# First-batch x by gathers of 128 rows, table zero fill on Scalar, and the second batch's first folds inside the first chunk

## The chip, the cores and the metric

The kernel runs on one core of one Trainium2 chip. The metric is the device time of one execution in microseconds (us), taken as the median over runs of the same program. Engines are named as in the profile: PE (TensorE, PEld its weight loads), DVE (VectorE), ACT (ScalarE), POOL (GpSimd) and SP (SyncE), which here only issues transfers. Transfers issued by SP and ACT go through hardware queues, those of POOL through a software queue.

## The reference

A Fourier mixing of x (8 batches, 3008 positions, 256 channels; the real part of a two-dimensional FFT over positions and channels), then a two-layer perceptron with a hard-swish in between.

```
X = np.fft.fft(x, axis=1)
X = np.fft.fft(X, axis=2)
x2 = X.real.reshape(B * S, D)
h = x2 @ w_in                       # 256 -> 2048
g = h * np.clip(h + 3.0, 0.0, 6.0) / 6.0
out = g @ w_out                     # 2048 -> 256
```

x is float32; both weights arrive as float64.

## The kernel before

**Tiling.** The FFT over 3008 = 47 x 64 positions is done in two stages of matmuls. Stage 1 transforms over the 47 rows. Because the transform of a real signal has symmetric and antisymmetric parts, x is first *folded*: a forward tile and a tile of mirrored partner rows are added (`fold_half`, `fold`), part 0 over the positions and part 1 over the channels. Stage 1's results z go to DRAM (`zd`, and a column `zq`) and come back in another layout as g; stage 2 multiplies g with a table T and gives q, which feeds the perceptron. One row of q is broadcast over the partitions through DRAM (`spread_half`, tile qn).

Batches go in pairs. The first pair is cut into two `Half` objects, `halves[0]` and `halves[1]`, one per batch, so that the first batch can start early. A half has four tiles m, taken in `ORDER` = 3, 0, 1, 2. Each has a forward tile `hb.x[m]` and a partner tile `hb.xr[m]`; the upper and lower 64 partitions hold two groups of columns, 47 rows each. The partner rows come by an indirect transfer, `gather`, whose row numbers lie in the integer tile IX (cast from the float tile FI). Forward rows come by two plain transfers of 64 or 48 rows each. Tile 3 is special: it has the last column group, and one more plain transfer wraps to column 0.

**Start.** Before the main loop the program clears buffers, loads the tables F, C, T and the first pieces of weights, makes float32 of the float64 weights, and does stage 1 of the first batch. Weights come in 16 pieces of 512 KB (`load_w`). `exponent_a` (ACT), `exponent_b` (a PE matmul) and `exponent_c` (ACT) make a piece's exponents, `mantissa` (DVE, two operations) its mantissa, and `join` (DVE) multiplies them. `fold_w_in` multiplies a w_in piece with the channel transform C on PE, ACT copies the result to W1, and SP copies one row of it to WN. `keep_awake` issues matmuls without use on PE. After the first two pieces come the four tiles of the first batch: `fold_half` on DVE, `stage1_early` on PE, copies of z by ACT. The half-empty diagonal blocks of T are zeroed by two memsets on POOL, and in tiles 0, 1, 2 a strip of partitions 32 to 63 is cleared by ACT before the load fills 47 rows of it, so that the rows that no transfer fills hold numbers.

Each engine executes its instructions in the order in which the program issues them; nothing reorders them. POOL's transfers use eight completion semaphores in turn, so each waits for the transfer eight before it; the hardware queues have a rotation of their own.

**Main loop.** The loop runs over `steps`: pair, chunk `ck` (12 per pair), and `fc` from 0 to 7. In each step PE does the first layer for a later step (`mlp1`, L520), DVE and ACT the activation (L529 to L569), POOL the sums `c` for the second layer (`combine`, three operations at L583 by a helper), and PE the second layer (`mlp2`, L613, three products with `a` and four with `c`), in a scheme with seven products of G blocks in place of eight. In the first chunk (`s` < 8) the weights are not ready, so `first_steps` and `second_steps` mix the weight work with the steps, and the second layer runs with eight products (`mlp2_first`, L593) that need no POOL. `mix_w_out(i)` on POOL makes the mixed G blocks for the second chunk on; it overwrites a block that `mlp2_first` reads.

**Background work.** `beside(p)` lists by hand what else is done at which step: `ahead` items are issued at the start of a step, `behind` items after `mlp1`. For pair 0 these are table loads, g loads, `stage2_half`, `spread_half`, the mixes, and all of the second batch: `take_half` and `load_half` (plain transfers on SP, gather on POOL), `fold_half` on POOL, and `stage1_quarters` on PE.

Pools are rings of buffers: `xpool` (4 buffers, also used by some weight pieces), `ypool` (2), `zpool` (2), `cpool` (3), `qpool` and `apool`.

Of the kernel before, what the change touches and what calls it, by code (L numbers as in the profile page):

```python
# [7 lines left out]
F32 = mybir.dt.float32  # L8
# [50 lines left out]
def kernel(  # L59
# [29 lines left out]
    NH = N2 // 2 + 1  # L89
    NG = NCK // 2  # L90
    NSG = 4
    DH = 32
    assert S == N1 * N2 and D == 2 * P and B % 2 == 0 and TB == 256 and NK1 % (2 * KK) == 0

# [19 lines left out]
    ctx.enter_context(tc.manual_schedule())  # L114

    F = consts.tile([P, 7 * PB], F32, name="F")
    FI = consts.tile([P, NP * NXC + 1], F32, name="FI")
    IX = consts.tile([P, NP * NXC], I32, name="IX")
    T = consts.tile([P, 2, NG, 2, 2 * KK, N2], F32, name="T")
    C = consts.tile([P, 2, D], F32, name="C")  # L120
    W1 = consts.tile([P, 2, FF], F32, name="W1")
# [15 lines left out]
    ORDER = [NM - 1] + list(range(NM - 1))  # L137

    def x_tile(pool=xpool, tag="x"):
        return pool.tile([PX, XC, D], F32, tag=tag, name="xt")  # L140

# [23 lines left out]
        pr.xr[c] = xr  # L167
        gather(xr, pr.p * NXC + c)

    def gather(xr, i):  # L170
        nc.gpsimd.indirect_dma_start(
            out=xr[0:PX].rearrange("p n d -> p (n d)"), out_offset=None, in_=x_r,
            in_offset=bass.IndirectOffsetOnAxis(ap=IX[0:PX, i:i + 1], axis=0),
        )

    class Half:
# [6 lines left out]
    def take_half(hb, m, pool=xpool, tag="x"):  # L183
        hb.x[m], hb.xr[m] = x_tile(pool, tag), x_tile(pool, tag)

    def load_half(hb, m, queue, gap=False):
        for h in range(2):
            c = m + h * NM
            nr = N1 + 1 if h or gap else PB
            n = XC if c < NXC - 1 else XC - 1  # L190
            rows, o = x_pn[hb.b * N1:hb.b * N1 + nr], hb.x[m][h * PB:h * PB + nr]
            queue.dma_start(out=o[:, 0:n, :], in_=rows[:, c * XC + 1:c * XC + 1 + n, :])
            if n < XC:
                queue.dma_start(out=o[:, n:XC, :], in_=rows[:, 0:1, :])
        gather(hb.xr[m], hb.b * NM + m)

    def fold_half(hb, m, part, eng):
        xt, xr = hb.x[m][0:PX - 1], hb.xr[m][0:PX - 1]
# [101 lines left out]
    def stage1_early(hb, m):  # L300
# [26 lines left out]
                    nc.tensor.matmul(ps[h][i * PB:(i + 1) * PB, :, to], table(t, h), y[rows(h), 2 * i:2 * i + 2, fr],  # L327
                                     start=(k == 0), stop=(k > 1), skip_group_check=True)
        k = ORDER.index(m)
        pool, tag = (zpool, "z") if k < 2 else (cpool, "c")  # L330
        z = pool.tile([PX, 2, 2, D + 1], F32, tag=tag, name="z")
        for h in range(2):
            nc.scalar.copy(z[:, h, :, D:], pt[h][0:PX])
# [13 lines left out]
    def stage1_quarters(hb, m):  # L347
        y = hb.y.pop(m)
        cosine, sine = slice(0, P + 1), slice(P + 1, D)
        ps = [bank([P, 2, D], "ps1"), ps_h.tile([P, 2, D], F32, tag="uv", name="ps1")]  # L350
        for i in range(2):
            for h in range(2):
                o = ps[h][i * PB:(i + 1) * PB]
                end = m == NM - 1 and h and i
                n = 1 if end else 2
                nc.tensor.matmul(o[:, 0:n], table(0, h), y[rows(h), 2 * i:2 * i + n], start=True, stop=not end,
                                 skip_group_check=True)
                for k, (j, cs) in enumerate([(XC - 1, cosine), (XC, cosine), (XC - 1, sine), (XC, sine)] if end else ()):
                    nc.tensor.matmul(o[:, 1, cs], table(k + 1, h), y[rows(h), j, cs], start=False, stop=(k % 2 == 1),
                                     skip_group_check=True)  # L360
        z = zpool.tile([PX, 2, 2, D], F32, tag="z", name="z")
        for h in range(2):
            nc.scalar.copy(z[:, h], ps[h][0:PX])
        zc = zpool.tile([PX, 2, 2], F32, tag="zc", bufs=4, name="zc")
        nc.scalar.activation(zc[:], z[:, :, :, P], AF.Identity, scale=FI[0:PX, NP * NXC:])
        if hb.b not in first.zd:
            first.zd[hb.b] = dpool.tile([NG, 2 * KK, 2, NS, D], F32, tag="zd1", name="zd")
            first.zq = dpool.tile([NG, 2 * KK, 2, NS], F32, tag="zq0", name="zq")
        zd, zq = first.zd[hb.b], first.zq
        for i in range(2):  # L370
            r = slice(i * PB, i * PB + PZ)
            for h in range(2):
                n0 = (m + h * NM) * XC + 2 * i
                end = m == NM - 1 and h and i
                n = 1 if end else 2
                nc.sync.dma_start(out=zd[:].rearrange("g k c n d -> (g k c) n d")[:, n0:n0 + 2, 0:D], in_=z[r, h])
                nc.sync.dma_start(out=zq[:, :, ::-1, n0:n0 + n].rearrange("g k c n -> (g k) c n"), in_=zc[r, h, 0:n])
                if end:
                    nc.sync.dma_start(out=zq[:, :, :, n0 + 1].rearrange("g k c -> (g k c)"), in_=z[r, h, 1, P])

    def turn_column(pr, c, z):
        zc = zpool.tile([PB + PZ, 2, 2], F32, tag="zc", bufs=4, name="zc")
        nc.scalar.activation(zc[:].rearrange("p n b -> p b n"), z[:, :, :, P], AF.Identity,
                             scale=FI[0:PB + PZ, NP * NXC:])
        for h in range(2):
            n = 1 if (c, h) == (NXC - 1, 1) else 2
            cs = slice(c * XC + 2 * h, c * XC + 2 * h + n)
# [441 lines left out]

    clear_bytes(0)  # L830
    nc.vector.memset(half[:], 0.5)
    nc.vector.tensor_copy(IX[:], FI[:, 0:NP * NXC])
    clear_bytes(1)
    clear_bytes(2)
    for k, m in enumerate(ORDER):
        take_half(hb, m, *((xpool, "x"), (xpool, "x"), (qpool, "q"), (apool, "a"))[k])
        if k:
            gap = hb.x[m][PB // 2:PB].rearrange("p n d -> p (n d)")
            nc.scalar.copy(gap.rearrange("p (i n) -> p i n", i=2), Z[PB // 2:PB].unsqueeze(1).to_broadcast([PB // 2, 2, 2 * TB]))

    def head(j):
        exponent_a(j)
# [20 lines left out]
                            channel_multiplier=1)  # L863
    nc.scalar.mul(E[:, 1], E[:, 0], -1.0)
    for k, m in enumerate(ORDER):
        load_half(hb, m, nc.gpsimd, gap=k > 0)
    for j in range(2, 4):
        load_w(j)
    for b in range(2):
        nc.gpsimd.memset(T[(1 - b) * N2:(2 - b) * N2, b].rearrange("p g a k n -> p (g a k n)"), 0.0)  # L870
    load_t(0)
    for j in range(2):
        exponent_a(j)
        mantissa(j)
        exponent_b(j)
        keep_awake(1)
    for j in range(2):
        tail(j)
        fold_w_in(j)
    keep_awake(1)  # L880
    for k, m in enumerate(ORDER):
        for part in range(2):
# [29 lines left out]
    def beside(p):  # L912
# [7 lines left out]
        if p == 0:  # L920
# [3 lines left out]
            put(4, stage2_half, halves[0], 1)  # L924
            put(5, spread_half, halves[0], 1)
            put(NF - 1, close_w)
            for i, t in enumerate((4, 6, 8, 9)):
                put(t, mix_w_out, i)
            for gr in range(2, NSG):
                put(8 * gr - 10, load_g_half, halves[0], gr)  # L930
# [2 lines left out]

            hb = halves[1]
            for k, m in enumerate(ORDER):
                t = 9 + 3 * k
                put(t - 3, take_half, hb, m)
                put(t - 3, load_half, hb, m, nc.sync)
                for part in range(2):
                    put(t + part, fold_half, hb, m, part, nc.gpsimd)  # L940
                put(t + 3, stage1_quarters, hb, m, at=behind)
            for gr in range(NSG):
                put(8 * gr + 23, load_g_half, hb, gr)
                put(8 * gr + 27 - (gr == 0), stage2_half, hb, gr)
# [132 lines left out]
def _tables(B, S, D):  # L1077
# [21 lines left out]

    npc = N2 // 8  # L1100
    row = np.zeros((128, B // 2, npc))
    for i in range(B):
        r = ((i * N1 + np.arange(N1)[::-1, None]) * 2 + 2) * npc - 1
        for h in range(2):
            if i > 1:
                row[i % 2 * 64:i % 2 * 64 + N1, i // 2] = r - np.arange(npc)
            else:
                row[h * 64:h * 64 + N1, 0, i * npc // 2:(i + 1) * npc // 2] = r - np.arange(npc // 2) - h * npc // 2
    sign = 1.0 - 2.0 * (np.arange(128)[:, None] % 2)
    f = np.concatenate([f1.reshape(128, -1), row.reshape(128, -1), sign], axis=1)  # L1110

    k = k1[:, None] + N1 * np.arange(N2)
    n2 = np.arange(N2 // 2) + 1
# [42 lines left out]
```

## Time and profile before

| | |
|---|---|
| median of 3 runs | 1953.43 us (1951.49 to 1958.76) |
| profiled execution | 1953.19 us, of it span 1951.5 us |
| granted PE clock over the span | 0.998 |
| PE busy | 1928.2 us (99%) |
| DVE busy | 1424.0 us (73%) |
| ACT busy | 678.2 us (35%) |
| POOL busy | 1440.9 us (74%) |
| read from and written to DRAM | 58.27 and 37.32 MB |
| PE waiting for POOL's `c` (L583), whole span | 2.6 us in 2 waits |
| POOL waiting for the first g (`see`) | 16.4 us in 1 wait |

The span is one execution taken by the profiler; the run's time lies 1.7 us above it. Busy time is an average over stages with different limits, so what a change in one stage is worth is read from that stage's own rows. Times within the span are counted from its start. A matmul in float32 is recorded as two instructions, so the counts of PE rows are twice those of the code.

### The profile page before, as it was taken

How to read it: one execution, taken by the hardware profiler on the slowest of the kernel's cores; microseconds unless marked ns; L12 is line 12 of the kernel's file. 1: busy time of each engine (PE TensorE's matmuls, PEld its weight loads, DVE VectorE, ACT ScalarE, POOL GpSimd, SP SyncE). 2: the span in 40 equal slices, each digit the busy share in tenths (PEclk: the TensorE clock that was granted, in tenths of full speed). 3: DMA queues.
4: the chain of work that ended last, by engine and by line, in shares of the span. 5: the costliest groups of instructions: out<-in, count | busy, mean ns of one | idle time of the engine just before them, and what ended most of it. 6: DMA issues, size and time to landing. Idle time of an engine off the chain costs nothing.

```text
span 1951.5 us, 28212 instructions
## 1 busy us (share of the span) xinstructions
PE 1928.2 (99%) x9354; PEld 1655.9 (85%) x9354; DVE 1424.0 (73%) x2754; ACT 678.2 (35%) x1166; POOL 1440.9 (74%) x1649
## 2 busy tenths in 40 slices
PE   8999999999999999999999999999999999999997
PEld 4678888888998888888898888888899888888887
DVE  4876776767777777777787777777778777777777
ACT  4633333333333333333333333333333333333322
POOL 4278888886677887787678887878667667666765
PEclk9999999999999999999999999999999999999999
DMA  6432223311112122121111221112110101101000
GB/s 179 153 86 65 67 52 91 77 47 35 34 33 55 44 68 73 40 55 27 41 32 46 57 57 42 51 50 54 35 28 20 28 17 26 30 17 28 19 19 20
DMA packets 154408, 97.43 MB, mean 50 GB/s; under 512 B 122035, under 2 KB 136174, under 8 KB 154262
## 3 DMA queue, kind: packets, MB, share of 16 engines
q1 hardware_dynamic: 143106, 59.71, 12.7%
q0 software_dynamic: 10448, 35.69, 6.6%
q8 instruction: 73, 1.20, 0.3%
q14 instruction: 73, 0.60, 0.1%
q10 hardware_dynamic: 708, 0.23, 0.1%
HBM read 58.27 MB, written 37.32 MB: 49 GB/s over the span
## 4 chain that ended last, share of the span: by engine, by line
PE 94%; DVE 2%; ACT 1%; POOL 1%; DMA 1%; issue 1%; DVEq 0%; ACTq 0%; POOLq 0%
PE acc L613 56%; PE v L520 16%; PE u L520 16%; PE ps L469 2%; PE ps L270 1%; PE acc L593 1%; DVE a L569 1%; PE awake L811 1%; ACT t L566 0%; DMA st<-in_moe_w_in_dram 0%; DVE s L529 0%; PE spare L794 0%; PE ps L327 0%; DVE o L674 0%; DVE u L550 0%
## 5 line engine op out<-in xcount | busy, mean ns | idle before, releaser
L583 POOL TENSOR_TENSOR c<-a 128x512 f32<-128x512 f32 (+1 forms) x375 | 468.3, 1249 | 370.4 <-PE acc L613 309.5
L613 PE MATMUL acc<-c,G 128*128 128x256 f32 (+1 forms) x3008 | 697.9, 375 | 2.7 <-POOL c L583 2.6
L566 ACT ACTIVATE t<-u,half 128x512 f32<-128x512 f32 (+1 forms) x384 | 260.8, 679 | 1144.5 <-DVE u L539 1065.3
L613 PEld LDWEIGHTS acc<-c,G 128*128 128x128 f32 x3008 | 564.9, 190 | 75.6 <-POOL c L583 4.7
L529 DVE SCALAR_TENSOR_TENSOR s<-qn,WN,u 128x256 f32<-128x256 f32 (+1 forms) x768 | 330.6, 472 | 346.5 <-PE u L520 342.0
L613 PE MATMUL acc<-a,G 128*128 128x256 f32 (+1 forms) x2256 | 541.8, 376 | 0.0
L613 PEld LDWEIGHTS acc<-a,G 128*128 128x128 f32 x2256 | 421.8, 190 | 72.9 <-issue 20.2
L520 PE MATMUL v<-q,W 127*128 127x256 f32 (+1 forms) x1536 | 389.4, 375 | 2.0 <-DVE a L569 2.0
L520 PE MATMUL u<-q,W 128*128 128x256 f32 (+1 forms) x1536 | 388.0, 375 | 0.2 <-ACT q L433 0.2
L569 DVE SCALAR_TENSOR_TENSOR a<-t,u 128x512 f32<-128x512 f32 (+2 forms) x448 | 264.0, 601 | 102.7 <-ACT t L566 99.4
L520 PEld LDWEIGHTS v<-q,W 127*128 127x128 f32 x1536 | 288.2, 190 | 42.8 <-ACT t L566 2.2
L520 PEld LDWEIGHTS u<-q,W 128*128 128x128 f32 x1536 | 285.9, 190 | 37.4 <-issue 2.4
L583 POOL TENSOR_TENSOR c<-a,c 128x256 f32<-128x256 f32 (+1 forms) x375 | 268.5, 716 | 29.4
L583 POOL TENSOR_TENSOR c<-c,a 128x256 f32<-128x256 f32 (+1 forms) x375 | 268.4, 716 | 29.4
L539 DVE TENSOR_TENSOR u<-s,v 128x512 f32<-128x512 f32 x352 | 245.1, 696 | 37.0 <-DVE s L529 0.5
L569 DVE SCALAR_TENSOR_TENSOR a<-t,v 128x512 f32<-128x512 f32 (+1 forms) x480 | 263.9, 567 | 0.3 <-ACT t L566 0.3
L566 ACT ACTIVATE t<-v,half 128x512 f32<-128x512 f32 (+1 forms) x384 | 260.4, 678 | 0.4 <-issue 0.3
L541 DVE TENSOR_TENSOR v<-v,s 128x512 f32<-128x512 f32 x352 | 244.1, 693 | 0.0
L583 POOL TENSOR_TENSOR r<-w,e 128x256 f32<-128x256 f32 (+1 forms) x92 | 88.8, 987 | 3.6
L623 ACT ACTIVATE e<-acc 128x512 f32<-128x512 f32 (+2 forms) x184 | 83.4, 544 | 0.0
L674 DVE STREAM_TRANSPOSE o<-r 128x256 f32<-128x256 f32 (+1 forms) x192 | 72.7, 416 | 0.5 <-POOL r L583 0.2
L583 POOL TENSOR_TENSOR w<-w,e 128x512 f32<-128x512 f32 (+1 forms) x46 | 57.5, 1250 | 3.6
(129 smaller groups left out, 784.1 us busy)
## 6 DMA issues: line engine op xcount, KB each, us to landing
out_dram<-o SPq DMA_DIRECT2D x747, 32.0 KB
g<-zd SPq DMA_DIRECT2D x42, 256.0 KB
zd<-z SPq DMA_DIRECT2D x48, 192.0 KB
xt<-in_x_dram POOLq DMA_DIRECT2D x22, 256.0 KB, 3.7
xt<-in_x_dram POOLq DMA_DIRECT2D x23, 192.0 KB, 4.1
st<-in_moe_w_in_dram POOLq DMA_DIRECT2D x8, 512.0 KB, 5.4
st<-in_moe_w_out_dram POOLq DMA_DIRECT2D x8, 512.0 KB, 7.8
qn<-qd SPq DMA_DIRECT2D x16, 256.0 KB
```

Of the source, the lines that this page charges most:

```text
L270: nc.tensor.matmul(ps[b][h * PB:(h + 1) * PB, 0:n], F[rows(b), 0:PB], y[rows(b), 2 * h:2 * h + n], start=True, stop=not last, skip_group_c ...
L469: nc.tensor.matmul(ps[:, blk, u * P:n].rearrange("p (b k) -> p b k", b=2), g[:, kk, blk * (P + 1):blk * (P + 1) + P], T[:, :, gr, blk, kk, ...
L520: nc.tensor.matmul(ps[:, i, 0:nq], W1[r, blk, f * P:(f + 1) * P], q[r, blk, of:of + nq], start=True, stop=True)
L529: nc.vector.scalar_tensor_tensor(s[:, i, 0:nq], qn[:, of:of + nq], WN[:, f:f + 1], u[:, i, 0:nq], op0=AL.mult, op1=AL.add)
L539: nc.vector.tensor_tensor(u[:], s[:], v[:], op=AL.add)
L541: nc.vector.tensor_tensor(v[:], v[:], s[:], op=AL.subtract)
L566: nc.scalar.activation(t, h, AF.Relu, bias=half[:], scale=scale)
L569: nc.vector.scalar_tensor_tensor(dst, t, 1.0, h, op0=AL.min, op1=AL.mult)
L583: (eng or nc.gpsimd).tensor_tensor(out, in0, in1, op=AL.add)
L613: nc.tensor.matmul(ch.acc[i // 2][:, i % 2, 0:ch.n], G[:, i, fc, :], mv, start=(fc == 0 and i % 2 == 0), stop=(fc == NF - 1), skip_group_c ...
L623: nc.scalar.mul(ch.e[:, k:i + 1, 0:ch.n], ch.acc[i // 2][:, 0:i + 1 - k, 0:ch.n], 1.0 / WS)
L674: nc.vector.transpose(o[:, 0:n // DH, h], ch.r[:, m, h, 0:n].rearrange("p (j i) -> p j i", i=DH))
```

## The change

Three groups of edits. Line numbers in this diff are its own.

1. *x of the first batch.* Tiles 0, 1, 2 get their forward rows by a gather too, of all 128 partitions, with an element offset of one position; the partner gathers of the first batch also take all 128 rows. IX and FI grow by four columns, and the unused rows get row numbers that lie inside x. The three strip clears on ACT are left out. Tile 3's forward rows stay plain transfers.
2. *Start order.* The zero fill of T moves from POOL to ACT, as two copies from a zero tile (`clear_table`): one in the place of the strip clears, one behind the exponents of the first two weight pieces. Both `exponent_c` are issued ahead of both `join` and `fold_w_in`. `load_t(0)` is issued behind these, so behind their WN transfers on SP.
3. *Second batch.* The steps of loading, folding and stage 1 move; the first tile's x goes to `cpool`; the mixes are called one step earlier; one early z goes to `ypool` in place of `cpool`.

```diff
-    def load_half(hb, m, queue, gap=False):
-        for h in range(2):
+    def load_half(hb, m, queue):
+        if hb.b == 0 and m < NM - 1:
+            gather(hb.x[m], NP * NXC + m, P, D)
+        for h in range(2 if hb.b or m == NM - 1 else 0):
...
-        gather(hb.xr[m], hb.b * NM + m)
+        gather(hb.xr[m], hb.b * NM + m, PX if hb.b else P)
...
-        pool, tag = (zpool, "z") if k < 2 else (cpool, "c")
+        pool, tag = ((zpool, "z"), (zpool, "z"), (ypool, "y"), (cpool, "c"))[k]
...
-        if k:
-            gap = hb.x[m][PB // 2:PB].rearrange("p n d -> p (n d)")
-            nc.scalar.copy(gap.rearrange("p (i n) -> p i n", i=2), Z[PB // 2:PB].unsqueeze(1).to_broadcast([PB // 2, 2, 2 * TB]))
+
+    def clear_table(b):
+        r = slice((1 - b) * N2, (2 - b) * N2)
+        t = T[r, b].rearrange("p g a k n -> p g (a k n)")
+        nc.scalar.copy(t, Z[r].unsqueeze(1).to_broadcast([N2, NG, 2 * TB]))
+
+    clear_table(0)
...
-    for b in range(2):
-        nc.gpsimd.memset(T[(1 - b) * N2:(2 - b) * N2, b].rearrange("p g a k n -> p (g a k n)"), 0.0)
-    load_t(0)
     for j in range(2):
         exponent_a(j)
         mantissa(j)
         exponent_b(j)
         keep_awake(1)
+    exponent_c(0)
+    exponent_c(1)
+    clear_table(1)
     for j in range(2):
-        tail(j)
+        join(j)
         fold_w_in(j)
+    load_t(0)
...
-            for i, t in enumerate((4, 6, 8, 9)):
+            for i, t in enumerate((3, 5, 7, 8)):
                 put(t, mix_w_out, i)
...
             for k, m in enumerate(ORDER):
-                t = 9 + 3 * k
-                put(t - 3, take_half, hb, m)
-                put(t - 3, load_half, hb, m, nc.sync)
+                put((1, 5, 8, 11)[k], take_half, hb, m, *((cpool, "c") if k == 0 else ()))
+                put((1, 5, 8, 11)[k], load_half, hb, m, nc.sync)
                 for part in range(2):
-                    put(t + part, fold_half, hb, m, part, nc.gpsimd)
-                put(t + 3, stage1_quarters, hb, m, at=behind)
+                    put((4, 6, 11, 14)[k] + part, fold_half, hb, m, part, nc.gpsimd)
+                put((8, 10, 15, 18)[k], stage1_quarters, hb, m, at=behind)
```

## The prediction

> **What bounds the kernel now.** I read the chain of waits first. By engine it is PE 94%, so nothing done elsewhere counts unless PE waits for it. Then I looked for the stretches where PE does not set the pace. There are two: the start up to about 44 us, and a gap around 125 us. From about 142 us to the end the PE rows stand back to back. In the lines below the columns are start, busy time, engine, line, operation, tiles, count, and in brackets the idle time before and what ended it.
>
> ```profile
> PE 94%; DVE 2%; ACT 1%; POOL 1%; DMA 1%; issue 1%; DVEq 0%; ACTq 0%; POOLq 0%
> ```
>
> The start, from the timeline:
>
> ```profile
> 16.24 0.59 ACT L796 COPY W<-wps 128x512 f32<-128x512 f32 x1 [2.80 <-PE wps L794]
> 16.72 0.59 ACT L745 ACTIVATE ex<-ex 128x512 int32<-128x512 f32 x1
> ...
> 17.35 0.69 DVE L762 TENSOR_TENSOR wi<-top,ex 128x512 f32<-128x512 f32 x1 [3.19 <-ACT ex L745]
> 17.95 0.55 DVE L206 TENSOR_TENSOR xt<-xt 111x381 f32<-111x381 f32 x1
> ...
> 19.95 5.36 POOL L870 MEMSET T<- 64x3072 f32 x2
> ...
> 21.26 1.36 DVE L223 COPY y<-xt 47x2 f32<-47x2 f32 x1
> ...
> 22.70 0.21 PE L312 MATMUL pt<-y,F 47*64 47x1 f32 x1 [1.54 <-DVE y L224]
> ...
> 26.14 0.69 DVE L206 TENSOR_TENSOR xt<-xt 111x508 f32<-111x508 f32 x1 [0.81 <-DMA xt<-in_x_dram,IX]
> ```
>
> Three things are to be seen. The second weight piece's `join` (L762) waits 3.19 us for an exponent that ACT computes only after copying the first piece's W, which waits for PE. The first x fold stands behind that join on DVE. Its last copies, of 47x2 elements, take 1.36 us and end at 22.62, when the first of POOL's two memsets ends (19.95 + 5.36/2). PE meanwhile idles, and its granted clock falls; in these rows by stage the clock is the third number from the end, the DMA share the next:
>
> ```profile
> 24.00:26.00 2.00, 2.00 (x7) 0.51 (x4) 1.33 (x4) 1.03 (x2) 1.31 (x1) 0.70 0.98 268
> 26.00:28.00 2.00, 2.00 (x27) 1.27 (x30) 1.37 (x3) 0.22 (x2) 0.00 (x0) 0.50 0.88 249
> 30.00:34.00 4.00, 4.00 (x65) 2.18 (x68) 0.00 (x0) 1.79 (x7) 0.00 (x0) 1.00 0.20 33
> ```
>
> The gap, from the timeline:
>
> ```profile
> 108.58 1.27 POOL L583 TENSOR_TENSOR c<-a 128x512 f32<-128x512 f32 x1 [23.49 <-DVE a L569]
> ...
> 120.47 1.00 POOL L206 TENSOR_TENSOR xt<-xt 111x381 f32<-111x381 f32 x1
> ...
> 124.17 1.28 POOL L583 TENSOR_TENSOR c<-a 128x512 f32<-128x512 f32 x1
> ...
> 125.50 2.31 PE L613 MATMUL acc<-c,G 128*128 128x256 f32 x8 [1.93 <-POOL c L583]
> ```
>
> POOL idles 23.49 us inside the first chunk, then has two weight mixes, a fold and a gather between combines, and PE waits for `c`. The five steps whose `mlp2` starts at 112.61 and 142.67 take 30.06 us. A bare step is 4.75 (142.67 to 147.43). One `stage2_half` adds 0.89 (171.89 to 172.78) and the first `stage1_quarters` 1.56 (from the end of L520 at 135.39 + 0.87 to 137.82). 23.75 + 0.89 + 1.56 = 26.20, so 3.9 us are stall.
>
> **The change, part by part**, in the times of the profile before.
>
> *Order of ACT and DVE.* Both exponents now precede the table fill and both W copies. ACT's exponent work on piece 1 ends at 12.96 and PE's matmul for it at 13.38, so `exponent_c(1)` ends near 14.0 and `join(1)` at 14.8 instead of 18.04. The two `fold_w_in` then run on PE without the 1.89 us gap before the second: 14.24 + 2 x 1.98 + one `keep_awake` of 0.86 = 19.1 for the first x matmul. The fold of that tile takes 3.35 us without the lock (17.95 to about 21.3); from 14.8, or from its gather's landing (issue 5.34 + 9.9 = 15.2), it ends by 18.6. So PE, not DVE, sets the start: 19.1. With PE no longer idle before it, I take full clock: tile 2.0, awake 1.06, 2.0, 1.06, 2.0, 1.06, 2.06 = 11.2, and the last x matmul ends at 30.3 instead of 35.3. That is 5.0 us.
>
> *Earlier weights.* `load_t(0)`, 256 KB, leaves the first microseconds for the place behind the WN writes. Until piece 1 landed at 11.46, 2.5 MB had moved (30 to 345 GB/s per 1.25 us slice); 0.26 MB less is about 1 us less. I take 0.8 (0 to 1.2), which moves the whole stage. The table is wanted at 42.4, so behind WN it has more than 10 us of cover.
>
> *Zero fill on ACT.* A 32x1024 copy took 1.04 us, so 3072 elements take about 3.1, twice. The first half (2.1 to 5.3) replaces three gap copies (2.94 us). The second, 14.0 to 17.1, delays the first W copy by 0.9 us; its WN rows are wanted at 45. Cost nothing. Removed with it is the POOL work that held L223.
>
> *x by gathers.* The three later tiles go from two plain transfers and a gather (2 x 0.55 + 0.98 = 2.1 us of POOL) to two gathers (2.0): even. The eight-deep rotation of POOL's transfers stays: transfer 10 waited 3.27 us for transfer 2. Bytes grow: seven gathers of 512 KB and 448 KB plain are 4032 KB of x against 3392. DMA share stood near 1.0 from 8 to 26 us at about 230 GB/s. If that rate stays, the 5.7 MB up to the last gather, plus the 0.6 MB that ran ahead of order before, are moved at about 27.2 us; fold 1.4 and matmuls 2.1 end at 30.7, so 1.2 later than the 29.5 that PE allows. At 250 GB/s it no longer shows. Bounds for a 128-row gather: the 64-row transfers' extra bytes (192 KB in 1.0 us between the next two lines) go at 197 GB/s, and the last tile would end near 35, leaving about 0; the 128-partition weight loads run at 318 to 403 GB/s (the last slices of the first 50 us), then PE decides.
>
> ```profile
> xt<-in_x_dram POOLq DMA_DIRECT2D x22, 256.0 KB, 3.7
> xt<-in_x_dram POOLq DMA_DIRECT2D x3, 64.0 KB, 2.7
> ```
>
> All 128 partitions are what the weight loads have, so I lean to that side and take 0.3 lost.
>
> The Trainium skill ("SBUF — State Buffer", section "Door 1") says that a transfer within partitions 0 to 63 reaches only 8 of 16 ports and one over all 128 reaches all. By it x would land well before PE asks, and the start would gain the full 5.8. This trace agrees in the order of the two rates above, but shows no 128-row gather.
>
> Start: 5.0 + 0.8 - 0.3 = 5.5 us; 0 to 6.3.
>
> *First folds inside the first chunk.* The tiles of the second batch are counted 1 to 4 here. The new homes (tile 1 in two `c` buffers, one early z in a `y` buffer) had their last user tens of us before, or none; `stage1_quarters` is the same PE work elsewhere; the mixes called one step earlier still wait for PE's last read of the blocks that they overwrite: nothing for the three. Fold 1 (2.6 + 3.6 us of POOL) moves into POOL's idle time: its x is asked for at step 1, SP issues it near 62.6, landing near 67; part 0 runs at 68.4 behind the first mix, part 1 behind the second at 84. Fold 2's plain loads stand on SP behind qn at 98.8, leave at 99.2 and land after the 4.1 us of the page's 192 KB rows: 104 to 104.5. On POOL behind fold 2's first part wait mix 3, its second part, `combine(8)`, mix 4, a gather and `combine(9)`. From 104: 2.5 + 3.2 + 2.7, so `combine(8)` runs 112.4 to 115.3; PE has 1.56 us of `stage1_quarters` ahead of it now and asks at 115.4: no wait. Mix 4 and the gather end at 119.5, the first op of `combine(9)` at 120.8; PE asks at 120.2. Stall left: 0.9 us with the third op. Later folds are single ones in steps with 5 us of lead. So 3.9 - 0.9 = 3.0 (0 to 3.9). SP gains 9 + 8 zd/zq issues ahead of out stores, about 0.75 us each; the qn row of chunk 2 then lands near 144.5 against 145.9 wanted: covered by 1.4 us.
>
> The Trainium skill (same page, "Who interferes with whom") speaks against this move: a DVE operation with two SBUF inputs, or one in its two-port mode, blocks while a GpSimd operation that reads SBUF runs. This trace shows only the 1.36 us copy beside a memset.
>
> Sum: 5.5 + 3.0 = 8.5 us. The profiled execution took 1953.19 us, 0.24 under the median of 1953.43 (span 1951.5 plus 1.7 around it): 1944.7.
>
> **Rivals.**
> (a) *x bound.* Gathers go at 200 to 230 GB/s and the last tile's landing sets the start. For: DMA share 1.0 and 640 KB more. Against: the weight loads' rate. Start gain 0 to 4.6, say 2: 1948.2.
> (b) *Mantissa blocked.* DVE's L753/L754 (0.42 and 0.69 us, pairs from 72.4 and from 89.2) meet POOL's fold operations of 1.0 to 1.27 us. For: the copy of 1.36 us above. Against: the folds end 1.2 us before 72.4 and 1.6 before 89.2. Two operations held: 2 us back, 1946.7.
> (c) *Slower: the fold ahead of the combines.* One late load on SP (fold 2's) holds POOL, and with it both mixes and the combines that PE reads. Each microsecond after 104 costs one: from 112.5 nothing is left of the gain, from 122 the kernel is over 0.5% slower. Against: SP then has only a qn wait of some 2 us ahead. For: SP stood idle 17 us at the first stores for want of data, so one wait of that kind suffices. At 117.5: 1958.
> (d) *No effect of the reorder at the start.* If something else gates the last x matmul at 35.3 (the `zd`-to-`g` path does not, it begins there), only 3.0 remain: 1950.2.
>
> **Numbers.** Forecast 0.62, (a) 0.14, (b) 0.12, (c) 0.08, (d) 0.04. A measurement here tells about 0.5%, 9.8 us: below 1943.7 is faster. The forecast's own range, 1942.5 to 1947, lies mostly above it; 0.27 of its 0.62 below (start near 6.3 and nearly the whole 3.9, or a stall that I have not counted). With (a), (b) and (d): same 0.66. Slower is most of (c): 0.07. Range 1941.8 to 1950.5: up to (d), leaving out (c) and the tail.
>
> **What would show it.** Right: `join(1)` near 14, first L312-type matmul near 18.5, no clock below 1.0 at 20 to 30 us, last x matmul near 30, the short DVE copies under 0.3 us; no 23 us POOL idle and PE's wait for `c` under 1 us in all. Wrong: x folds waiting on the gathers by over 1 us; POOL waiting on an x load with `combine(8)` behind it; L753 or L754 over 1 us; DVE waiting for qn at chunk 2.

## The result, and the profile after

The changed kernel takes 1943.70 us (median of 7 runs, 1942.76 to 1944.77) against 1953.43 us for the kernel before (7 runs, 1949.64 to 1959.66): a ratio of 0.9947, 95% interval 0.9931 to 0.9962. By this ratio it is 0.53% faster, by the two medians 0.50%. That it is faster is clear; whether by more than the 0.5% (9.8 us) that the prediction names is not, since the interval spans that bound. The profiled execution took 1943.62 us with a span of 1941.9 us, 9.6 us less than the span of 1951.5 us before. In the changed kernel the lines named here lie three lower than before (the fold's L206 is L209, `combine`'s L583 is L586, `mlp2`'s L613 is L616).

By the chain of waits the kernel is bound as before:

```profile
PE 93%; DVE 3%; ACT 1%; DMA 1%; POOL 1%; issue 1%; SPq 0%; DVEq 0%; ACTq 0%; POOLq 0%
```

So the 9.6 us are again to be looked for where PE does not set the pace. First the start, from the timeline of the changed kernel:

```profile
9.32 0.43 DVE L756 TENSOR_SCALAR top<-st 128x512 int32<-128x512 int32 x1 [1.92 <-DMA st<-in_moe_w_in_dram]
...
11.32 1.29 DVE L765 TENSOR_TENSOR wi<-top,ex 128x512 f32<-128x512 f32 x2 [0.84 <-ACT ex L748]
11.76 2.74 ACT L844 COPY T<-Z 64x3072 f32<-64x3072 f32 x1
12.06 3.72 PE L797 MATMUL wps<-wi,C 128*128 128x256 f32 x16
...
15.83 0.17 DVE L226 COPY y<-xt 47x2 f32<-47x2 f32 x1
15.89 0.17 DVE L227 COPY y<-xt 47x2 f32<-47x2 f32 x1
...
16.57 0.29 PE L312 MATMUL pt<-y,F 47*64 47x2 f32 x8
...
20.07 0.69 DVE L209 TENSOR_TENSOR xt<-xt 111x508 f32<-111x508 f32 x1 [1.23 <-DMA xt<-in_x_dram,IX]
```

Both joins are one group of two now, without the 3.19 us between them, and the two `fold_w_in` (L797) run as one block of 16 matmuls. The short copies take 0.17 us. The first x matmul starts at 16.57 instead of 20.87 us. The second weight piece, whose mantissa operation began at 11.48 us before, is there at 9.32. Of the folds one waits for a gather, 1.23 us, in the time of another tile's matmuls. PE now keeps its clock; in the rows by stage (same columns as before) it is the third number from the end:

```profile
24.00:26.00 2.00, 2.00 (x30) 0.79 (x26) 0.00 (x0) 1.18 (x4) 0.00 (x0) 1.00 0.35 55
26.00:28.00 2.00, 2.00 (x33) 1.15 (x26) 0.29 (x1) 0.45 (x3) 0.00 (x0) 1.00 0.39 63
```

Then the gap, from the same timeline:

```profile
97.81 1.26 POOL L209 TENSOR_TENSOR xt<-xt 111x508 f32<-111x508 f32 x1 [16.53 <-DMA xt<-in_x_dram]
...
105.81 1.26 POOL L586 TENSOR_TENSOR c<-a 128x512 f32<-128x512 f32 x1
107.08 1.56 PE L616 MATMUL acc<-a,G 128*128 128x256 f32 x6
...
108.48 1.89 PE L616 MATMUL acc<-c,G 128*128 128x256 f32 x8
...
114.24 2.31 PE L616 MATMUL acc<-c,G 128*128 128x256 f32 x8 [0.85 <-POOL c L586]
```

Fold 2 begins when its x has landed, `combine(8)` stands behind it and is still in time for PE, and one wait of 0.85 us for `c` is left at `combine(9)`, where there were 2.6 us.

Three stretches of the span show where the time went. They are cut at two PE rows that every kernel here has: the first `stage2_half` matmul and the first `mlp2` matmul that uses mixed blocks (step 8). One `stage1_quarters` of 1.56 us moved from the third stretch to the second; the last two columns are without it.

| us | start, to `stage2_half` | first chunk, to `mlp2` of step 8 | rest | first chunk without the moved work | rest without it |
|---|---|---|---|---|---|
| before | 42.39 | 70.22 | 1838.9 | 70.22 | 1838.9 |
| after | 34.77 | 72.31 | 1834.8 | 70.75 | 1836.4 |
| gain | 7.6 | | | -0.5 | 2.5 |

### The profile page after: what moved, and what is told of

Its sections match the earlier page's. It is cut to its first block, busy times and chain, and to the rows that moved or that the text cites. A ratio compares the mean times of both kernels' runs of the same rounds, so it can differ in the third digit from the quotient of the medians.

```text
span 1941.9 us, 28190 instructions
## 1 busy us (share of the span) xinstructions
PE 1924.4 (99%) x9354; PEld 1659.3 (85%) x9354; DVE 1423.9 (73%) x2754; ACT 680.7 (35%) x1165; POOL 1435.6 (74%) x1644
## 4 chain that ended last, share of the span: by engine, by line
PE 93%; DVE 3%; ACT 1%; DMA 1%; POOL 1%; issue 1%; SPq 0%; DVEq 0%; ACTq 0%; POOLq 0%
PE acc L616 56%; PE v L523 16%; PE u L523 16%; PE ps L472 2%; PE ps L273 1%; DVE a L572 1%; DVE s L532 1%; PE awake L814 1%; ACT t L569 1%; DMA st<-in_moe_w_in_dram 0%; DVE o L677 0%; DVE u L553 0%; PE ps L433 0%; POOL c L586 0%; PE ps L330 0%
## 5 line engine op out<-in xcount | busy, mean ns | idle before, releaser
L586 POOL TENSOR_TENSOR c<-a 128x512 f32<-128x512 f32 (+1 forms) x375 | 468.1, 1248 | 355.5 <-PE acc L616 319.9
L616 PE MATMUL acc<-c,G 128*128 128x256 f32 (+1 forms) x3008 | 697.9, 375 | 0.9 <-POOL c L586 0.8
L616 PEld LDWEIGHTS acc<-c,G 128*128 128x128 f32 x3008 | 566.6, 191 | 71.5 <-POOL c L586 2.1
L616 PE MATMUL acc<-a,G 128*128 128x256 f32 (+1 forms) x2256 | 542.1, 376 | 0.0
L616 PEld LDWEIGHTS acc<-a,G 128*128 128x128 f32 x2256 | 422.9, 190 | 71.9 <-issue 20.2
L586 POOL TENSOR_TENSOR c<-c,a 128x256 f32<-128x256 f32 (+1 forms) x375 | 268.3, 715 | 29.4
L586 POOL TENSOR_TENSOR c<-a,c 128x256 f32<-128x256 f32 (+1 forms) x375 | 268.3, 715 | 29.4
L586 POOL TENSOR_TENSOR r<-w,e 128x256 f32<-128x256 f32 (+1 forms) x92 | 88.8, 986 | 3.6
L586 POOL TENSOR_TENSOR w<-w,e 128x512 f32<-128x512 f32 (+1 forms) x46 | 57.5, 1249 | 3.6
```

The source lines that it names most:

```text
L586: (eng or nc.gpsimd).tensor_tensor(out, in0, in1, op=AL.add)
L616: nc.tensor.matmul(ch.acc[i // 2][:, i % 2, 0:ch.n], G[:, i, fc, :], mv, start=(fc == 0 and i % 2 == 0), stop=(fc == NF - 1), skip_group_c ...
```

## The experiments

The experiments ran in three groups, each on one chip; on these the kernel before had medians of 1953.96, 1950.29 and 1954.71 us; the changed kernel's own 1943.70 was taken apart from these, beside the 1953.43. So a ratio compares with the kernel before on the same chip, while differences of 1 us between kernels of different groups are read from the stretches, not from the medians. The same cuts for all kernels, one profile each, with the landing of the second weight piece (piece 2, by the start of its mantissa operation):

| kernel | piece 2 | start | first chunk | rest | median us | ratio to before (95%) |
|---|---|---|---|---|---|---|
| before | 11.48 | 42.39 | 70.22 | 1838.9 | 1953.43 | |
| after | 9.32 | 34.77 | 72.31 | 1834.8 | 1943.70 | 0.9947 (0.9931 to 0.9962) |
| gathers alone | 11.99 | 41.30 | 69.96 | 1839.0 | 1952.97 | 1.0001 (0.9985 to 1.0018) |
| order alone | 9.03 | 34.75 | 69.32 | 1839.0 | 1946.61 | 0.9967 (0.9955 to 0.9978) |
| folds alone | 11.66 | 45.60 | 71.64 | 1835.4 | 1954.15 | 1.0001 (0.9981 to 1.002) |
| after, 112 rows | 9.30 | 35.13 | 72.23 | 1834.8 | 1944.12 | 0.9953 (0.9939 to 0.9967) |
| after, 64-row halves | 9.92 | 37.40 | 72.09 | 1834.8 | 1945.96 (1 run) | |
| after, plain x | 9.90 | 35.44 | 71.72 | 1834.7 | 1944.06 | 0.9969 (0.9958 to 0.9981) |
| after, table first | 10.70 | 36.13 | 71.70 | 1835.4 | 1944.61 | 0.9972 (0.9962 to 0.9981) |
| after, no filler | 9.80 | 31.55 | 71.31 | 1835.1 | 1939.99 | 0.9952 (0.9935 to 0.9968) |
| after, tiles 1 and 2 earlier | 9.18 | 34.63 | 71.41 | 1833.7 | 1941.27 | 0.9957 (0.9941 to 0.9974) |
| after, tile 1 earlier | 10.32 | 35.76 | 70.88 | 1835.0 | 1943.31 | 0.9939 (0.9917 to 0.9961) |
| after, tile 2 earlier | 9.32 | 35.13 | 72.36 | 1833.4 | 1942.75 | 0.9936 (0.9914 to 0.9958) |
| after, no filler, both earlier | 10.46 | 32.18 | 71.20 | 1833.7 | 1938.42 | 0.9915 (0.9898 to 0.9932) |

### One group of edits at a time

**Gathers alone** (kernel before, forward rows by 128-row gathers, strip clears left out).

```diff
+        if hb.b == 0 and m < NM - 1:
+            gather(hb.x[m], NP * NXC + m, P, D)
+        for h in range(2 if hb.b or m == NM - 1 else 0):
...
+        gather(hb.xr[m], hb.b * NM + m, PX if hb.b else P)
```

> The kernel before with the gathers of 128 rows alone (order of the start, zero fill on POOL and second batch as before). Theory: the 128-row gathers speed up the x phase, so the DMA rate from 10 to 20 us is near 400 GB/s (220 to 250 before), the second weight piece lands near 10 us (11.46 before, 9.32 with the whole change) and the last gather near 21 us (26.1 before); but join(1) still waits for the W copy and the short DVE copies can still be held by the memset, so the last x matmul ends at 33 to 34 us (35.3 before, 27.7 with the whole change): 1951 to 1952. Rival (the table load that moved away made the weights land early): the second piece at 11.4, last x matmul at 35: 1953.

No change that can be measured, with an interval of 3 us to each side; of the two expected values the rival's 1953 is the nearer. The folds no longer waited for x, but the second weight piece landed at 11.99 us, no earlier than before, and PE's order set the end of the start stage. In this profile the granted clock fell early, to 0.74, 0.50 and 0.91 in the three 2 us slices from 12 to 18 us, so its start stretch contains some of that loss.

**Order alone** (kernel before, with the exponents ahead of the joins, `clear_table` on ACT, and `load_t(0)` behind).

```diff
+    clear_table(0)
...
-    load_t(0)
...
+    exponent_c(0)
+    exponent_c(1)
+    clear_table(1)
     for j in range(2):
-        tail(j)
+        join(j)
         fold_w_in(j)
+    load_t(0)
```

> The kernel before with the new order of the start alone (exponents first, zero fill on ACT, table load behind WN); x by plain transfers and 112-row gathers, second batch as before. Theory: the order gives about 5 us of the start and the moved table load some 0.5 to 1; the DMA rate stays at 220 to 250 GB/s, the second piece lands near 10.5 to 11, the last gather near 25 to 26 and the last x matmul ends at 29 to 30 us; short DVE copies of 47x2 take under 0.3 us; no clock under 1.0 at 20 to 30 us. 1947 to 1948. Rival (the whole start gain comes from the faster gathers): last x matmul at 33 or later, 1951 or more.

This is the largest part: the median fell by 7.3 us and the start stretch is as short as in the whole change, though with plain x two folds waited 1.8 us each for their gathers. The profiled execution, 1944.83 us, is the fastest of its ten, so its stretches lie on the short side. PE still waited 2.6 us for `c`.

**Folds alone** (kernel before, with only the third group of edits: the steps of the second batch, the mixes one step earlier, the two new buffers).

```diff
-                t = 9 + 3 * k
...
+                put((1, 5, 8, 11)[k], load_half, hb, m, nc.sync)
...
+                    put((4, 6, 11, 14)[k] + part, fold_half, hb, m, part, nc.gpsimd)
+                put((8, 10, 15, 18)[k], stage1_quarters, hb, m, at=behind)
```

> The kernel before with the new steps of the second batch alone (with the mixes one step earlier and the two new buffer homes). Theory: the gap at 112 to 143 us gives back 2.3 us, and POOL's first fold holds DVE's mantissa operations (L753 and L754 at 0.9 to 1.2 us in place of 0.42 and 0.69) for a loss of about 0.5: 1951.2 to 1951.8, last x matmul at 35.3 as before. Rival (the gap's gain needs the earlier start): 1953.

By the median nothing was gained, with an interval of 4 us to each side. In the profiled execution the granted clock stayed at 0.50 to 34 us, so that its start stretch is 3.2 us longer than that of before, and in this execution that outweighs what came after; a gain of 2 us would not show in an interval that wide. From the profile of this run, by stage:

```profile
24.00:26.00 2.00, 2.00 (x7) 0.71 (x4) 2.00 (x6) 1.03 (x2) 1.31 (x1) 0.55 0.91 296
26.00:28.00 2.00, 2.00 (x21) 1.01 (x24) 0.66 (x2) 0.22 (x2) 0.00 (x0) 0.50 0.53 105
28.00:30.00 2.00, 2.00 (x24) 0.99 (x16) 0.00 (x0) 0.00 (x0) 0.00 (x0) 0.50 0.00 0
30.00:34.00 4.00, 4.00 (x30) 1.63 (x30) 0.00 (x0) 1.29 (x4) 0.00 (x0) 0.50 0.20 32
```

The rest stretch is free of that: 1835.4 us with the folds moved, 1838.9 to 1839.0 in the three kernels without. Of these 3.5 us, 1.56 are the `stage1_quarters` that only moved, so 1.9 are gained, where 2.3 were expected. The first chunk without the moved work is 70.1, no longer than the 70.2 of before.

### How x comes

**112 rows** (changed kernel, first-batch gathers over 112 rows).

```diff
-            gather(hb.x[m], NP * NXC + m, P, D)
+            gather(hb.x[m], NP * NXC + m, PX, D)
...
-        gather(hb.xr[m], hb.b * NM + m, PX if hb.b else P)
+        gather(hb.xr[m], hb.b * NM + m, PX)
```

> The changed kernel with its gathers of the first batch over 112 rows in place of 128 (12% fewer bytes). Theory (the span of 128 partitions makes the rate): the DMA rate from 10 to 20 us falls to 230 to 270 GB/s, the last gather lands at 24 us or later (19.9 in the changed kernel), the second piece at 10 or later (9.3), the last x matmul ends 0.5 to 2 us later: 1944.3 to 1946. Rival (gathers as such, or fewer transfers, make the rate): 400 GB/s stays, the last gather lands by 19.5, 1943.7.

The rate did fall, and the time did not follow. From the view of the DMA queues, 11 to 21 us, first the changed kernel, then this one: total, mean rate, and the gathers with their median time from issue to landing.

```profile
DMA packets 1310, 4.03 MB, mean 403 GB/s; under 512 B 327, under 2 KB 327, under 8 KB 1310
...
xt<-in_x_dram,IX POOLq DMA_INDIRECT x3, 7.0
```

```profile
DMA packets 737, 2.65 MB, mean 265 GB/s; under 512 B 89, under 2 KB 89, under 8 KB 737
...
xt<-in_x_dram,IX POOLq DMA_INDIRECT x3, 9.7
```

The first line counts all transfers of the stretch. The kind of gather is the same and its bytes differ by an eighth, so it is the 16 rows more that make the rate. Two folds then waited 1.90 and 2.02 us for x, and `stage2_half` came 0.4 us later, no more.

**Plain x** (changed kernel without the gathers: order and folds only; the edit is the reverse of the first one).

> The changed kernel without its first group: x of the first batch by plain transfers and 112-row gathers, strips cleared by ACT as before; new order of the start and new steps of the second batch kept. Theory (PE's own order sets the end of the start, and the faster gathers are hidden): last x matmul at 27.5 as with the change, last gather landing near 22.7, 1943.5 to 1944.5. Rival (the gathers carry a part): 1945 or more.

Within 1 us of the changed kernel by every stretch, and 0.4 us by the median. Folds waited for gathers again, three times and 4.9 us in all, 2.10 for the last one; `stage2_half` came 0.67 us later with a weight piece that landed 0.58 us later.

**64-row halves** (changed kernel, forward rows of a whole tile in two plain transfers of 64 rows).

```diff
-            gather(hb.x[m], NP * NXC + m, P, D)
+            for h in range(2):
+                c = m + h * NM
+                queue.dma_start(out=hb.x[m][h * PB:(h + 1) * PB], in_=x_pn[0:PB, c * XC + 1:(c + 1) * XC + 1, :])
```

> The changed kernel with the forward rows of tiles 0, 1, 2 loaded by two plain transfers of 64 partitions each in place of one gather of 128 partitions; the partner gathers stay at 128. Theory: it is the number of partitions in one transfer that makes the rate, so the stretch from 11 to 20 us falls from 400 to 416 GB/s to some 250 to 320, and the time stays within 0.5 us of the changed kernel because x is waited for by PE's order, not by the rate. Rival: it is the kind of transfer (gather against plain with short rows), or the odd row count, that held the rate before; then 64-row plain transfers side by side keep 400.

The fall of the rate was right, the time was not: 210 to 272 GB/s in slices of 1.25 us from 11 to 20 us, four folds waited 7.1 us in all, and `stage2_half` came 2.6 us later, of which the later weight piece explains 0.6. In this run, 2 us of rival (a) are seen. So with all 128 rows asked for, the transfers' form is worth about 2 us, by one profile; but the kernel before asked for fewer bytes, and with these the plain form is as good. The rival's wording was unclear on which form should keep 400; the run shows only that two 64-row transfers don't.

### What the earlier start is made of

**Table first** (changed kernel, `load_t(0)` in its old place).

```diff
         load_w(j)
+    load_t(0)
     for j in range(2):
         exponent_a(j)
...
-    load_t(0)
```

> The changed kernel with load_t(0) issued in its old place, ahead of the first weight work, in place of behind WN. Theory (the table's two transfers, 64 partitions each, hold back the second weight piece in the transfer engines): the second piece lands at 11 to 12 us (9.3 in the changed kernel, 9.0 with the new order alone, 11.46 to 11.99 wherever the table is first), everything behind shifts, the last x matmul ends 2 to 2.5 us later (29.5 to 30): 1945.5 to 1946.5. Rival (it is the order of ACT and DVE alone): 9.5 us, 1943.7.

Less than was expected: piece 2 lands at 10.70 instead of 9.32 us, 1.38 later, and `stage2_half` comes 1.36 us later. The weights do set the start, microsecond by microsecond: in four kernels whose piece 2 lands between 9.18 and 10.70 us (changed, table first, tile 1 earlier, both tiles earlier), `stage2_half` follows it by 25.43 to 25.45 us. How much of the 1.38 is the table's is less sure. The six kernels with the start order of the changed one and its gathers of 128 rows have piece 2 at 9.18 to 10.46 us, 9.73 in the mean; against these, table first is 0.2 to 1.5 us later, 1.0 against the mean.

**No filler** (changed kernel without the `keep_awake` between x tiles).

```diff
-        if k < NM - 1:
-            keep_awake(1)
```

> The changed kernel without the three keep_awake matmuls between the four x tiles of the first batch (they compute nothing that is used). Theory (in the changed kernel PE's own queue sets this stretch, the fillers are on the path at 1.06 us each, and the folds are ready): the last x matmul ends at 24.5 to 25 in place of 27.5: 1940.5 to 1941.5. Rival (without them PE idles and its granted clock falls): clock under 1.0 between 20 and 40 us, no gain or a loss.

The x tiles ran back to back with the clock at 1.00 throughout, and `stage2_half` came 3.2 us earlier. With the new order these matmuls hold up PE, and the clock did not need them. The median is 0.5 us under what was expected; the first chunk is 1.0 us shorter too, for which see the last run below.

### The folds in the first chunk

The first chunk of the changed kernel is 1.4 us longer than that of the kernel with the new order alone (70.75 without the moved work, against 69.32). The timeline of the changed kernel:

```profile
64.67 0.99 POOL L209 TENSOR_TENSOR xt<-xt 111x381 f32<-111x381 f32 x1 [3.95 <-DMA xt<-in_x_dram]
64.89 1.07 DVE L756 TENSOR_SCALAR top<-st 128x512 int32<-128x512 int32 x1
...
65.63 1.04 POOL L210 TENSOR_TENSOR xt<-xt 111x381 f32<-111x381 f32 x1
65.99 1.23 DVE L757 SCALAR_TENSOR_TENSOR top<-st,top 128x512 f32<-128x512 uint32 x1
66.64 0.90 POOL L209 TENSOR_TENSOR xt<-xt 47x127 f32<-47x127 f32 x1
...
67.99 0.87 DVE L756 TENSOR_SCALAR top<-st 128x512 int32<-128x512 int32 x1
...
75.25 0.58 ACT L436 COPY q<-ps 128x512 f32<-128x512 f32 x1
...
75.88 0.59 PE L745 MATMUL ex<-PM,E 128*128 128x512 f16 x2 [1.46 <-ACT q L436]
```

Fold 1 waited 3.95 us for its x and so came to lie beside the mantissa pairs. Alone these operations take 0.42 and 0.69 us; here 1.07 and 1.23, then 0.87 beside a weight mix that stood behind the fold on POOL. DVE is then late with the activation, ACT with its copy of q, and PE waits 1.46 us. Two kernels moved the loads (`take_half`, left out of the cuts here, and `load_half`) one step earlier in the list, apart, and a third both together.

**Tile 1 earlier.**

```diff
...
-                put((1, 5, 8, 11)[k], load_half, hb, m, nc.sync)
+                put((0, 5, 8, 11)[k], load_half, hb, m, nc.sync)
```

> The changed kernel with the second batch's tile 1 alone asked for at step 0 instead of step 1; fold 2 stays late. Theory: fold 1 part 0 then runs before the mantissa pair, L756 and L757 near step 2 fall back to 0.4 and 0.7 us, and the first chunk gets back the 0.5 us that it lost: 1943.2. Rival: the 0.5 us are the longer path of stage1_quarters among the steps, not the mantissa: 1943.7, with short mantissa operations and no gain.

```profile
61.68 1.00 POOL L209 TENSOR_TENSOR xt<-xt 111x381 f32<-111x381 f32 x1
...
65.75 0.42 DVE L756 TENSOR_SCALAR top<-st 128x512 int32<-128x512 int32 x1
66.21 0.69 DVE L757 SCALAR_TENSOR_TENSOR top<-st,top 128x512 f32<-128x512 uint32 x1
...
74.81 0.58 ACT L436 COPY q<-ps 128x512 f32<-128x512 f32 x1
...
75.44 0.59 PE L745 MATMUL ex<-PM,E 128*128 128x512 f16 x2
```

Same lines in its timeline: the fold is done before the mantissa begins, the operations are short, and PE's row has no wait. One step in the list is much in time: SP issued these loads from 32.5 us on instead of 55.07. The first chunk is 1.43 us shorter, and without the moved work it is 69.32, exactly that of the kernel with the new order alone. The median shows only 0.4 of that; in the profiled run the first chunk began 1.0 us later, with its weight piece.

**Tile 2 earlier.**

```diff
...
-                put((1, 5, 8, 11)[k], load_half, hb, m, nc.sync)
+                put((1, 4, 8, 11)[k], load_half, hb, m, nc.sync)
```

> The changed kernel with tile 2 alone asked for at step 4 instead of step 5; fold 1 stays late and beside the mantissa. Theory: fold 2 leaves POOL before combine(8) and PE's wait of 0.85 us for c goes, worth about 1 us, with the rest of the 2.4 us of the run with both edits from combine(8) onward: 1941.8 to 1942.7. Rival: fold 2 comes to lie beside a mantissa pair as it did with both edits, and what the gap gives is lost there: 1943.5 or more.

PE's waits for `c` were gone altogether, and the rest stretch was 1.4 us shorter. Fold 2 ran at 81.24 us with a mantissa pair of 1.34 and 1.10 us beside it, as the rival had it, but this added nothing to the first chunk (72.36 against 72.31). The median, 1942.75, lies just above the range that was expected. Without the moved work the rest stretch is 1835.0, 3.9 us under before: the whole stall that the prediction had summed.

**Both earlier.**

```diff
...
-                put((1, 5, 8, 11)[k], load_half, hb, m, nc.sync)
+                put((0, 4, 8, 11)[k], load_half, hb, m, nc.sync)
```

> The changed kernel with the second batch's tile 1 asked for at step 0 in place of 1 and tile 2 at step 4 in place of 5. Theory (the first fold, run late because its x lands late, holds DVE's mantissa operations, and the second, waiting 16.5 us for its x, holds the combines): fold 1 runs at about 61 us ahead of the mantissa operations, whose durations return to 0.42 and 0.69; fold 2 starts near 95 in place of 97.8; PE's wait for c falls from 0.8 to near 0. Gain 1 to 2 us: 1941.7 to 1942.7. Rival (the earlier loads delay the weights, or the held mantissa has cover): 1943.7 or more.

Both gains came together: 0.9 us in the first chunk and 1.1 in the rest, and the median is 0.4 us under the range that was expected. Fold 2 ran at 80.91 us, not near 95, and again met a mantissa pair (1.42 and 1.46 us). The 0.5 us by which this first chunk exceeds that with tile 1 alone lies before that: PE waits 0.47 us for q at 74.84, behind a pair of 0.52 and 1.10 us that ran from 69.69 on, beside a weight mix on POOL at 69.85.

**No filler, both earlier** (the edits of these two kernels together).

> The changed kernel with both edits that won alone: tile 1 of the second batch asked for at step 0 and tile 2 at step 4, and no keep_awake between the first batch's x tiles. Theory: they lie in different stretches (folds at 60 to 116 us, fillers at 16 to 28 us) and add: 2.4 + 3.7 = 6.1 us under the changed kernel, so some 1937.6 us, span near 1936. Rival 1: with x tiles back to back the first chunk begins 3.2 us earlier while x of the second batch comes no earlier, so a fold slides back onto the mantissa pairs or ahead of combine(8), and 1 to 2 us of the 2.4 are lost: 1939 to 1940. Rival 2: the granted clock falls without the fillers, and the start gives the 3.2 us back: above 1940.

1938.42 us, 0.85% under the kernel before and the fastest here. It is 0.8 us above what was expected. The 3.7 us of the run without fillers already held 1.0 us of first chunk (71.31 against 72.31): there fold 1 began 1.4 us ahead of its mantissa pair, at 60.14 us, the pair took 0.68 and 1.19 us, and PE waited 0.57 us for q where it had waited 1.46. Adding both gains counted that twice. 2.4 + 3.7 - 1.0 gives 1938.6. In the profiled run the start is also 0.6 us longer than without fillers alone, with a weight piece that landed 0.7 us later.

## Why the prediction was right

The time, 1943.70, is 1.0 us under the forecast of 1944.7 and inside its own range. The mechanisms are the predicted ones, the closeness is in part luck: the start was worth 2.1 us more than the 5.5 predicted, and a first-chunk loss of 0.5 and a gap smaller by 0.5 took about half of that back. All four signs that the prediction named as wrong are there too: a fold waits 1.23 us for its gather, POOL waits 16.53 us for an x load with `combine(8)` behind it, mantissa operations take 1.07 and 1.23 us, and DVE waits 2.00 us for qn. The second and the third cost time: 1.4 us are left of the gap, where 0.9 was in the sum, and the mantissa takes 1.4.

**Order of ACT and DVE, 5.0 us: right.** The exponents first bring the joins together and `fold_w_in` into one block. The kernel with the order alone has the whole gain of the start, the one with the gathers alone only 1.1 us of its start stretch and nothing in its time (with a clock loss of its own in the profile), so rival (d) falls. Of the 7.6 us, 2.1 go with the earlier weights, which leaves 5.5 for the order. The step from piece 2 to the first x matmul is 7.25 us (9.32 to 16.57), where the prediction had 11.46 to 19.1, or 7.64.

**Earlier weights, 0.8 us: the term that was mis-sized.** In the two profiles compared, piece 2 landed 2.1 us earlier (11.48 to 9.32), outside the 0 to 1.2 taken; against the mean of the six kernels with this start (9.73) it is 1.75. The estimate for the table, 0.26 MB at the mean rate or about 1 us, is not refuted: the run with the table first gives 0.2 to 1.5. The rest stays open. That run has piece 2 at 10.70, the three kernels with the old order at 11.48 to 11.99, and no run tells which of the other edits to the start makes this difference.

**Zero fill on ACT, nothing: right.** The fill takes 2.74 us at 11.76, beside PE's `fold_w_in`, and the first W copy follows at 14.40 us; PE and DVE have no wait for it in the trace. The short copies on DVE fell from 1.36 to 0.17 us. They do so with the memsets kept and only earlier, too: in the run with the gathers alone the two memsets start at 17.44, end at 22.80, and the copies at 22.94 take 0.17.

**x by gathers, -0.3 us: right in effect, the choice of bound too.** The 128-row gathers run at 400 GB/s and more, the upper bound, but this is not what holds x: at 112 rows the folds waited 3.9 us in two waits and the start lost 0.4. The gain from this group of edits is 0 to 0.7 us; of the 0.67 by which the start with plain x is longer, 0.58 go with its weight piece. Rival (a) is refuted for the change itself; the run with 64-row halves shows what it looks like, with waits of 7.1 us.

The Trainium skill ("SBUF — State Buffer", "Can I just issue two DMAs to hit both halves?") says that two transfers, one on each half, serialize and do not reach all ports. This trace agrees in the run with halves: 210 to 272 GB/s where one transfer of 128 rows has 400. By the port table of the same page ("Door 1") 112 rows reach every port as well; here they ran at 265, so that rule does not tell the rate of 112 rows.

**First folds, 3.0 us: gap right, 2.5 measured.** Fold 2's x was used at 97.81 us; moved by the 7.6 us of the earlier start, the predicted 104 is 96.4. `combine(8)` made no wait, and the wait left at `combine(9)` is 0.85 where 0.9 was predicted. The stall itself was 3.9 us as summed, since the kernel with tile 2 earlier gets all of it back; 1.4 of it is left here. So rival (c) did not come about: nothing on SP held fold 2's loads. DVE did wait 2.00 us for qn at 139.67 us, so the cover of 1.4 us was not there. PE has no wait from 120 to 240 us in the trace, so it cost nothing.

**Mantissa blocked, rival (b): it happened as well, and the prediction gave it as an alternative.** "The folds end 1.2 us before 72.4" rested on x landing in time. Moved by 7.6 us, the prediction had the loads issued near 55.0 and x there near 59.4. They were issued from 55.07 to 56.24 us, but x was there only at 64.67: the step that failed is the 4.4 us from issue to landing, which became 8.4 from the last issue. Four weight pieces were asked for on POOL from 52.12 to 56.84 us, and the DMA engines were full from 58 us until x had landed; by stage, the share is the last number but one:

```profile
58.00:61.00 3.00, 1.82 (x8) 1.18 (x7) 2.85 (x5) 2.98 (x6) 2.49 (x4) 1.00 1.06 265
61.00:64.00 3.00, 3.00 (x9) 1.22 (x8) 2.74 (x6) 1.78 (x4) 0.00 (x0) 1.00 1.03 253
```

The price was 1.4 us, by the kernel with tile 1 earlier, where 2 was named. It follows PE's wait for q, 1.46 us here and none there. The net loss is only 0.5, because a wait of before that the prediction had not seen went away in return: there DVE waited 0.79 us for a WN row, and PE 1.03 for the q copy behind it, from the timeline of the kernel before (the kernel with the new order alone has neither wait, and its first chunk is 0.9 us shorter):

```profile
79.77 0.48 DVE L529 SCALAR_TENSOR_TENSOR s<-qn,WN,u 128x256 f32<-128x256 f32 x1 [0.79 <-DMA WN<-W]
...
82.96 0.59 PE L742 MATMUL ex<-PM,E 128*128 128x512 f16 x2 [1.03 <-ACT q L433]
```

The Trainium skill ("SBUF — State Buffer", "Who interferes with whom") has this as a lock: a DVE operation with two SBUF inputs, or in a two-port mode, blocks while a GpSimd operation that reads SBUF runs, and the reverse. The rows agree on both sides: DVE's 0.42 and 0.69 became 1.07 and 1.23, and POOL's operation of 47x127 took 0.90 where it takes 0.44 in the run with tile 1 earlier.

In sum, against the kernel before: +7.6 at the start, -1.4 by the mantissa, +0.9 by the wait that went, +2.5 in the gap, 9.6 us.

## What to carry to other kernels

Time a transfer's landing by what else the DMA engines carry at that moment, not by its median elsewhere: x of fold 1 took 8 us instead of 4 among four weight pieces, and asking for it one step earlier in the hand-written order was worth 1.4 us of the first chunk. When the first weights set the start, look at what else is loaded in front of them, and take several profiles before pricing it: with the same start the second piece landed anywhere from 9.18 to 10.46 us. And when an idle time has been taken out, go back to what had been put there to fill it: the filler matmuls cost 3.2 us, more than the moved folds gained.

## What the hardware showed that was not expected

With gathers of 128 rows the transfers moved 400 to 416 GB/s (in slices of 1.25 us from 11.25 to 18.75 us), with gathers of 112 rows 262 to 272, in the same place of the same kernel; the gathers landed 7.0 and 9.7 us after issue.

Without the filler matmuls the granted clock stayed at 1.00 from 14 to 34 us, with PE busy for 19.0 of these 20 us. In all three profiles with the old order it fell to 0.50: from about 24 to 28 us in before, from 24 to beyond 34 us with the folds alone, and near 14 to 16 us with the gathers alone. The runs of before scatter over 10 us (1949.64 to 1959.66), those of the kernels with the new order over 0.8 to 3.5. The scatter goes with the clock: of the 54 runs of before taken beside the experiments, the 15 with a mean granted clock of 0.995 or less took 1953.96 to 1961.05 us, the 34 with 0.997 or more 1948.17 to 1954.74; every run of a kernel with the new order has 0.997 or more. With the new order most of the scatter is gone. Why the clock falls in some runs and not in others is not shown.

The collision of two operations lengthens both of them, and what it costs the kernel depends on what stands behind: 1.4 us at fold 1, next to nothing at fold 2, with mantissa operations lengthened by about as much (1.34 and 1.10 us in the kernel with tile 2 earlier).
